# Where two batches' products wait between SBUF and DRAM, and which engine rounds weight blocks: one change to a three-stage kernel on one core

## The chip, the core and the metric

The kernel runs on one core of a Trainium2 chip. The metric is the device time of one execution in microseconds, the median of several. Five engines work side by side, each on its own list of instructions in order: PE (TensorE, the matrix products), ACT (ScalarE), DVE (VectorE), POOL (GpSimd) and SP (SyncE), which here issues every DMA.

## The reference

Three layers follow one another on 4 batches of 448 tokens.

- Attention with a sigmoid: `attn = sigmoid(q kT / 8 - log 448)` for 12 heads of 64, then `attn @ v`. The heads side by side give x, 1792 x 768.
- A gated product: `a = x @ w_a`, `b = x @ w_b` (both 768 x 1536), then `(a * b) @ w_out` (1536 x 768).
- Soft mixture of experts: `logits = x @ phi` (32 slots). A softmax over all tokens (`d`) mixes tokens into slots, 8 experts apply `relu(slot @ w1) @ w2`, and a softmax over the slots (`c`) gives the result, 1792 x 768.

The kernel never forms the second layer's output: it multiplies w_out with phi for the logits, and mixes the tokens of g = a * b into slots before w_out. So of g three things are needed per batch: g times (w_out phi), g with tokens on partitions, and the sum over tokens of `d` times g.

## The kernel before

**Stages.** Attention runs over 24 pairs of heads, six pairs a batch. While it runs, the weights are rebuilt from 64-bit words and written to DRAM as `ab32` and `out32`. Batch 0's product a * b (`ab(0)`) is woven into attention. Batches 1 and 2 are multiplied together by a scheme with 7 products in place of 8 (`unit(u)`, 12 units, line 682). Batch 3 follows in `ab(3)`, line 516. The tail reads out32 and the experts' weights w1 and w2 and ends with the output.

**Two roundings for each operand.** PE multiplies a number as a rounded high part and a remainder: an engine casts `t` to the high part, and another engine subtracts it from `t`. In the units `block` does this for the seven weight blocks (lines 571 and 572): even blocks are cast by DVE, odd ones by ACT, and POOL subtracts. `late_operands` (line 623) makes four operands at the start of the units; ACT casts and DVE subtracts (line 594). `last_x` does the same for batch 3's x, DVE casting, POOL subtracting (lines 633, 634).

**The last product, `ab(3)`.** It has 24 halves: 12 blocks of 128 columns, for w_a and then for w_b. A half is 18 matmuls on PE, in three steps of six. Its weight block comes from `ab32` (384 KB, `wr<-ab`) two halves ahead; DVE casts it (line 433), POOL subtracts (line 434), and the freed place lets SP issue the load of the block two halves later (line 425). At step 6, six steps into `ab(3)`, the pools of the units are closed and a pool `e1` of 17 load slots of 1 MB opens in their place; `pump` issues one load for the tail into the next open slot at every third step.

**g with tokens on partitions.** `group(b, gi)` (line 459) transposes a third of a batch's g into a tile. Batch 1 and 2 each own one half of `gk_01`; every third is written to DRAM (`gk32`, line 497) before the next third overwrites it. `reload_gk(b)` (line 500) reads the three thirds of one batch back into both halves of `gk_01` and into `gk_2`.

**The batch step `LG(b)`** (line 760) is a generator; PE's work is interrupted for one piece of it at a time, after a step of six matmuls. Its pieces are the logits (line 714), two token transposes (line 748) and `dg` (line 757), the sum over tokens. `LG(1)` and `LG(2)` run in `ab(3)`: the reload for batch 1 is asked for at step 12, that for batch 2 at the end of `LG(1)`, because both use the same tiles.

SP issues in program order. A DMA that waits for a tile to come free holds back all that stand behind it.

```
        for gi in range(3):
            t = (gk_01[:, gi] if gi < 2 else gk_2)[:T]
            sp.dma_start(out=t, in_=gk32[b - 1, gi])
```

Of the kernel before, what the change touches and what calls it, by code (L numbers as in the profile page):

```python
# [9 lines left out]
F32 = mybir.dt.float32  # L10
# [10 lines left out]
C = 4  # L21
T = S // C
# [4 lines left out]
NE1, NE2 = 17, 4  # L27
# [6 lines left out]
def body(ctx, tc, q, k, v, w_a, w_b, w_out, phi, w1, w2, out):  # L34
    nc = tc.nc
    pe, act, dve, pool, sp = nc.tensor, nc.scalar, nc.vector, nc.gpsimd, nc.sync
# [5 lines left out]
    gkp = ctx.enter_context(tc.tile_pool(name="gkp", bufs=1, side="left"))  # L42
# [5 lines left out]
    pools = {}  # L48
    drp = ctx.enter_context(tc.tile_pool(name="drp", bufs=1, space=bass.MemoryType.DRAM))
    psp = ps_ctx.enter_context(tc.tile_pool(name="psp", bufs=1, space=PSUM))  # L50

    run = {}
# [22 lines left out]
    gk_01 = lgp.tile([128, 2, 2048], F32, name="gk_01")  # L75
    gk_2 = gkp.tile([128, 2048], F32, tag="gkp0", name="gk_2")
# [10 lines left out]
    ab32 = drp.tile([KF, 2, 128, KD * 128], F32, name="ab32")  # L87
    out32 = drp.tile([128, KF, DM], F32, name="out32")
    clog32 = drp.tile([T, C, B, NS], F32, name="clog32")
    gk32 = drp.tile([2, 3, T, 2048], F32, name="gk32")  # L90

    idj = ident.rearrange("p (j s) -> p j s", j=4)
    small = gk_01.rearrange("p a n -> p (a n)")
# [104 lines left out]
    xt = {}  # L198
# [250 lines left out]
    gT, gtok, live = {}, {}, set()  # L449
# [9 lines left out]
    def group(b, gi, evac=(act.copy, dve.tensor_copy) * 2):  # L459

        if (b, gi) != (B - 1, 2):
            for _ in range(GDEL):
                yield
        lps = lp[b]
        t = ms()
        for j in range(4):
            fc = 4 * gi + j
            pe.matmul(t[32 * j:32 * j + 32], wphi[:, fc], gT[b, fc], start=True, stop=True)  # L468
        if gi == 0:
            act.copy(lps, t)  # L470
        else:
            dve.tensor_tensor(lps, lps, t, op=ALU.add)
        if (b, gi) == (B - 1, 2):
            gk = e2.tile([128, 2048], F32, tag="e20", name="gk_3")
        elif b in (1, 2):
            gk = gk_01[:, b - 1]
        else:
            gk = gk_01[:, gi] if gi < 2 else gk_2
        gkt = gk[:T]
        gk = gk[:T].rearrange("p (c n) -> p c n", c=C)  # L480
        if (b, gi) == (B - 1, 2):
            yield
        for c in range(C):
            tp = ms((T, 512))
            for i in range(4):
                pe.transpose(tp[:, i * 128:(i + 1) * 128],  # L486
                             gT[b, 4 * gi + i][:, c * T:(c + 1) * T], ident)
            evac[c](gk[:, c], tp)
            if c != 1 or (b, gi) == (B - 1, 2):
                yield  # L490
                if b < B - 1 and c < C - 1:
                    yield
        for i in range(4):
            gT.pop((b, 4 * gi + i))
            live.discard(b * KF + 4 * gi + i)
        if b in (1, 2):
            sp.dma_start(out=gk32[b - 1, gi], in_=gkt)
        gtok[b, gi] = gk

    def reload_gk(b):  # L500
        for gi in range(3):
            t = (gk_01[:, gi] if gi < 2 else gk_2)[:T]
            sp.dma_start(out=t, in_=gk32[b - 1, gi])
            gtok[b, gi] = t.rearrange("p (c n) -> p c n", c=C)

    def ab(b):
        for fc in range(KF):
# [58 lines left out]
    def block(u, m, t):  # L566
        q = (7 * u + m) % RING
        abt = {4: "wh0", 5: "wl0", 6: "wh1", 7: "wl1"}
        nm = abt.get(q, f"wx{q}")
        w = (abp if q in abt else pools["cp"]).tile([128, 2, BLK], F32R, tag=nm, name=nm)  # L570
        (act.copy if m % 2 else dve.tensor_copy)(w[:, 0], t)  # L571
        pool.tensor_tensor(w[:, 1], t, w[:, 0].bitcast(F32), op=ALU.subtract)  # L572
        wb_t[u, m] = w

# [16 lines left out]
    def split_x(nm, i, t, pl, names, rnd=None, sub=None):  # L591
        xh, xl = (pl.tile([128, S], F32R, tag=x, name=x) for x in names)
        (rnd or dve.tensor_copy)(xh, t)
        (sub or pool).tensor_tensor(xl, t, xh.bitcast(F32), op=ALU.subtract)
        xs[nm, i] = xh, xl
# [24 lines left out]
    def late_operands(nm):  # L620
        n = {"S3": NP, "S1": 2 * NP, "A22": 2 * NP + 3, "S4": NP + 3}[nm]
        for i in range(3):
            split_x(nm, i, xt[n + i], pools["xb"], (f"{nm}h{i}", f"{nm}l{i}"), act.copy, dve)

    def last_x():

        for kk in range(NP):
            g = 3 * NP + kk
            r = xt[g]
            xh = x1p.tile([128, S], F32R, tag=f"t{kk}", name=f"t{kk}")  # L630
            nm = f"t{kk + 5 if kk else 11}"
            xl = x1p.tile([128, S], F32R, tag=nm, name=nm)
            dve.tensor_copy(xh, r)
            pool.tensor_tensor(xl, r, xh.bitcast(F32), op=ALU.subtract)
            xt[g] = (xh, xl)
            yield
# [75 lines left out]
    def logits(b):  # L712
        lf, lps = ms(), lp[b]
        pe.matmul(lf, selF.rearrange("p j s -> p (j s)"), lps, start=True, stop=True)
        yield
        mx = col()
        dve.tensor_reduce(mx, lf, axis=AX.X, op=ALU.max)
        nm = col()
        if b:
            mn = col()  # L720
            dve.tensor_tensor(mn, run["m"], mx, op=ALU.max)
            mx, m0 = mn, run["m"]
        dve.tensor_scalar(nm, mx, -1.0, None, op0=ALU.mult)
        if b:
            dm = col()
            dve.tensor_tensor(dm, m0, mx, op=ALU.subtract)
        run["m"] = mx
        yield
        sm = col()
        ls, d = run["lsd"]  # L730
        act.activation(d, lf, AF.Exp, bias=nm, accum_out=sm)
        if b:
            al = col()
            act.activation(al, dm, AF.Exp)
            run["al"] = al
        act.copy(ls, lf)
        yield
        if b:
            sn = col()
            dve.scalar_tensor_tensor(sn, run["s"], al, sm, op0=ALU.mult, op1=ALU.add)  # L740
            sm = sn
        run["s"] = sm
# [7 lines left out]

    def dg(b, dtok, gp, groups):

        gk = gtok[b, 2][:, None] if groups == (2,) else gk_01[:T].rearrange("p g (c n) -> p g c n", c=C)
        o = gp.rearrange("p (g n) -> p g n", g=3)[:, groups[0]:groups[-1] + 1]
        for c in range(C):
            for j in range(4):
                pe.matmul(o[32 * j:32 * j + 32], dtok[:, c], gk[:, :, c, j * 128:(j + 1) * 128],  # L757
                          start=(c == 0), stop=(c == C - 1))

    def LG(b):  # L760
        t = run["lsd2"]
        run["lsd"] = t[:, :S], t[:, S:2 * S]
        dtok, ltok = (t[:T, i:i + C * NS].rearrange("p (c s) -> p c s", c=C) for i in (2 * S, 2 * S + C * NS))
        yield
        yield from logits(b)
        run["lg"] = b
        yield
        tokens(run["lsd"][0], ltok)
        sp.dma_start(out=clog32[:, :, b], in_=ltok)
        yield  # L770
        tokens(run["lsd"][1], dtok)
        yield
        gp = ms((128, FF // 4))
        for groups in ((0, 1), (2,)):
            dg(b, dtok, gp, groups)
        if b:
            dve.scalar_tensor_tensor(acc, acc, run["al"], gp, op0=ALU.mult, op1=ALU.add)
        else:
            dve.tensor_copy(acc, gp)
        yield  # L780
        if b == B - 3:
            reload_gk(b + 1)
        elif b == B - 2:
            run.pop("lsd2")
            open_slots(run["e1"], [1])
            open_slots(gkp, [0])

    def last_LG():

# [69 lines left out]
    def open_slots(pl, names):  # L859
        slots.extend((pl, f"{pl.name}{i}") for i in names)  # L860
# [104 lines left out]
    for i, frac in enumerate(ab(B - 1)):  # L965
        fc = i // 6
        if i < 6:
            fill_step()
        if i == 6:
            while fill:  # L970
                fill_step()
            cp_ctx.close()
            xb_ctx.close()
            e1 = run["e1"] = ctx.enter_context(tc.tile_pool(name="e1", bufs=1, side="right"))
            run["lsd2"] = e1.tile([128, 2048], F32, tag="e11", name="lsd2")
            run["wr"] = e1.tile([128, 2048], F32, tag="e10", name="wr")
            load_w(LAST + 6)
            load_w(LAST + 7)
            open_slots(e1, range(2, NE1))
            fill.append(LG(1))  # L980
            fill.append(LG(2))
        elif i == 12:
            reload_gk(1)
        if i > 6 and i % 3 == 1:
            pump()
    for kk in range(NP):
# [19 lines left out]
    for what in order0:  # L1006
        i = what[1]
        h, n, f0 = (0, 4, 4 * i) if i < 3 else (1, 6, 6 * (i - 3))
# [8 lines left out]
    for kk in range(0, KD, 2):  # L1017
        f = ms((128, 2, 256))
# [8 lines left out]
    for n in range(0, len(order1), 4):  # L1027
        _, g, x, _ = order1[n]
# [12 lines left out]
    for kk in range(0, KE, 2):  # L1041
        f = ms((128, 2, 256))
# [30 lines left out]
    for h in range(2):  # L1073
        for b in range(B):
            pl, nm = slots.pop(0)
# [4 lines left out]
    for h, (c0, w) in enumerate(COLS):  # L1080
# [4 lines left out]
        t = ms((128, w))  # L1085
        pe.matmul(t, selF.rearrange("p j s -> p (j s)"), s4[:, c0:c0 + w], start=True, stop=True)
        evac[h](s4r[:, c0:c0 + w], t)
        for c in range(C):
            op = []
            for b in range(B):  # L1090
                tag = tags[k % 6]
# [35 lines left out]
```

## Time and profile before

| | |
|---|---|
| median of 3 runs | 725.8 us (725.58 to 730.64) |
| the profiled execution's own time | 728.99 us |
| its span | 727.1 us |
| granted TensorE clock, mean | 0.975 |
| PE busy | 665.9 us (92%) |
| DVE, POOL, ACT busy | 392.3, 301.2, 285.2 us |
| the 16 DMA engines, mean share | 64.5% |

The profiled execution is 1.89 us longer than its span, and 3.2 us longer than the median. A busy PE is not a fast PE: its matmuls overlap, and the granted clock (1.0 stands for 2.4 GHz, 0.5 for 1.2 GHz) sets their pace. DMA shares are means over 16 engines and can read a few hundredths above 1.

### The profile page before, as it was taken

How to read it: one execution, taken by the hardware profiler on the slowest of the kernel's cores; microseconds unless marked ns; L12 is line 12 of the kernel's file. 1: busy time of each engine (PE TensorE's matmuls, PEld its weight loads, DVE VectorE, ACT ScalarE, POOL GpSimd, SP SyncE). 2: the span in 40 equal slices, each digit the busy share in tenths (PEclk: the TensorE clock that was granted, in tenths of full speed). 3: DMA queues.
4: the chain of work that ended last, by engine and by line, in shares of the span. 5: the costliest groups of instructions: out<-in, count | busy, mean ns of one | idle time of the engine just before them, and what ended most of it. 6: DMA issues, size and time to landing. Idle time of an engine off the chain costs nothing.

```text
span 727.1 us, 10908 instructions
## 1 busy us (share of the span) xinstructions
PE 665.9 (92%) x4123; PEld 473.6 (65%) x4123; DVE 392.3 (54%) x580; ACT 285.2 (39%) x503; POOL 301.2 (41%) x226
## 2 busy tenths in 40 slices
PE   6999998999999999999899999999299999998683
PEld 3547876776774545468788988988178987433131
DVE  4767897889725246249997887754022222300022
ACT  4987887877825666761113112103011011100021
POOL 0244677677634066016986676643124442100000
PEclk9999999999999899999999999999799999998898
DMA  9998998899624242101114313325998995999998
GB/s 205 254 285 210 290 322 295 248 305 279 218 66 147 55 102 64 57 0 45 45 44 137 95 49 106 121 81 157 286 276 316 356 345 202 365 415 416 410 356 258
DMA packets 105332, 150.58 MB, mean 207 GB/s; under 512 B 50944, under 2 KB 83968, under 8 KB 100864
## 3 DMA queue, kind: packets, MB, share of 16 engines
q1 hardware_dynamic: 105280, 149.89, 64.5%
q8 instruction: 33, 0.54, 0.3%
q14 instruction: 19, 0.16, 0.1%
HBM read 124.53 MB, written 25.34 MB: 206 GB/s over the span
## 4 chain that ended last, share of the span: by engine, by line
PE 71%; DMA 13%; DVE 9%; ACT 3%; issue 2%; SPq 0%; POOL 0%; ACTq 0%; DVEq 0%; POOLq 0%
PE ab L516 22%; PE sc L195 11%; PE sc L682 10%; DMA e<-in_moe_w 8%; PE sc L182 7%; PE ab L682 5%; PE ms L149 3%; PE ms L486 2%; DMA gk<-gk 2%; PE ms L757 2%; PE ab L182 1%; DMA ab<-w 1%; DMA gkp<-in_moe_w 1%; PE ms L468 1%; ACT a L185 1%
## 5 line engine op out<-in xcount | busy, mean ns | idle before, releaser
L339 POOL TENSOR_TENSOR w<-gk,cy 128x768 int32<-128x768 int32 x36 | 66.6, 1850 | 91.3 <-DVE gk L334 57.6
L185 ACT ACTIVATE a<-sc,sums 112x448 f32<-112x448 f32 x158 | 89.1, 645 | 14.0 <-PE sc L182 13.9
L195 PE MATMUL sc<-a,vn 112*64 112x448 f32 x384 | 77.8, 546 | 2.3 <-ACT a L185 2.3
L434 POOL TENSOR_TENSOR wl<-wr,wh 128x768 fp32r<-128x768 f32 x22 | 40.5, 1842 | 76.9 <-DVE wh L433 41.2
L516 PE MATMUL ab<-t,wh 128*128 128x448 f32 x288 | 64.9, 370 | 0.0
L516 PEld LDWEIGHTS ab<-t,wh 128*128 128x128 f32 x288 | 53.2, 188 | 4.6 <-issue 0.6
L195 PEld LDWEIGHTS sc<-a,vn 112*64 112x64 f32 x384 | 25.7, 136 | 40.5 <-issue 34.0
L434 POOL TENSOR_TENSOR wl<-w,wh 128x768 fp32r<-128x768 f32 x24 | 45.0, 1876 | 2.5 <-ACT wh L433 2.5
L1058 PE MATMUL ab<-e,gk 128*32 128x384 f32 x240 | 34.0, 558 | 9.8 <-DMA e<-in_moe_w 9.8
L332 DVE TENSOR_SCALAR mf<-gk 128x768 f32<-128x768 f32 x36 | 34.1, 946 | 16.4 <-ACT gk L321 16.4
L523 ACT COPY misc<-ab 128x448 f32<-128x448 f32 x24 | 12.9, 536 | 76.5 <-PE ab L516 76.5
L572 POOL TENSOR_TENSOR wx<-wr,wx 128x384 fp32r<-128x384 f32 x29 | 34.8, 1206 | 12.5 <-DVE wx L571 12.5
L571 ACT CAST wx<-T 128x384 fp32r<-128x384 f32 x23 | 11.5, 512 | 69.1 <-DVE T L587 42.1
L182 PE MATMUL sc<-qh,kh 64*112 64x448 f32 x158 | 36.5, 432 | 1.3 <-ACT qh L142 0.6
L526 DVE TENSOR_TENSOR misc<-misc,ab 128x448 f32<-128x448 f32 x24 | 14.8, 617 | 38.1 <-PE ab L516 38.1
L333 DVE TENSOR_SCALAR gk<-mf 128x768 uint32<-128x768 uint32 x36 | 34.3, 953 | 1.2
L516 PE MATMUL ab<-xh,wh 128*128 128x448 f32 x144 | 34.9, 378 | 0.0
L516 PE MATMUL ab<-xh,wl 128*128 128x448 f32 x144 | 34.5, 375 | 0.0
L516 PE MATMUL ab<-xl,wh 128*128 128x448 f32 x144 | 34.5, 375 | 0.0
L516 PE MATMUL ab<-t,wl 128*128 128x448 f32 x144 | 34.0, 371 | 0.0
L572 POOL TENSOR_TENSOR wx<-T,wx 128x384 fp32r<-128x384 f32 x23 | 25.3, 1102 | 16.0 <-ACT wx L571 16.0
L182 PE MATMUL sc<-qh,kl 64*112 64x448 f32 x158 | 31.8, 375 | 0.0
(421 smaller groups left out, 1455.9 us busy)
## 6 DMA issues: line engine op xcount, KB each, us to landing
e<-in_moe_w SPq DMA_DIRECT2D x23, 1024.0 KB, 7.5
e<-in_moe_w SPq DMA_DIRECT2D x23, 768.0 KB, 15.1
wr<-ab SPq DMA_DIRECT2D x14, 768.0 KB, 4.6
gk<-gk SPq DMA_DIRECT2D x12, 896.0 KB, 7.8
ab<-w SPq DMA_DIRECT2D x24, 384.0 KB, 7.2
wr<-ab SPq DMA_DIRECT2D x18, 384.0 KB, 5.4
kn<-in_k SPq DMA_DIRECT2D x48, 112.0 KB, 4.1
qn<-in_q SPq DMA_DIRECT2D x48, 112.0 KB, 4.1
```

Of the source, the lines that this page charges most:

```text
L149: pe.transpose(t[:, c * T:(c + 1) * T], a[:, c].rearrange("p h d -> p (h d)"), ident[:T, :T])
L182: pe.matmul(sc[h], kx[r, cs], qx[r], start=(i == 0), stop=(i == 2))
L185: act.activation(a, sc[h], AF.Sigmoid, bias=nlog[:T], scale=1.0 / math.sqrt(D))
L195: pe.matmul(pv_t[g][64 * h:64 * h + 64], qkv_t["v", g][:, h, c, :], a_t.pop((g, h, c)), start=(c == 0), stop=(c == C - 1))
L332: dve.tensor_scalar(mf, m, LOW, HIGH, op0=ALU.max, op1=ALU.min)
L333: dve.tensor_scalar(mi, mf.bitcast(U32), 3, 0x3FFFFFFF, op0=ALU.logical_shift_left, op1=ALU.bitwise_and)
L339: pool.tensor_tensor(thirds(w), m.bitcast(I32), thirds(cy_t.pop(x)), op=ALU.add)
L434: pool.tensor_tensor(wl, t, wh.bitcast(F32), op=ALU.subtract)
L516: pe.matmul(t, w[:, kk * 128:(kk + 1) * 128], xt[b * NP + kk][xi], start=(s == 0 and kk == 0), stop=(s == 2 and kk == KD - 1))
L572: pool.tensor_tensor(w[:, 1], t, w[:, 0].bitcast(F32), op=ALU.subtract)
L682: pe.matmul(t, w[:, wi, k * 128:(k + 1) * 128], xs[ORDER[m], k][xi], start=(s == 0 and k == 0), stop=(s == 2 and k == 2))
L1058: pe.matmul(sps[h][32 * j:32 * j + 32], hT[:, 2 * x + i, 2 * j + g], ring[order2[n + j]][0][:, i, c0:c0 + w], start=(g == 0 and x == 0 and ...
```

## The change

Of batches 1 and 2 the last third of g is no longer written to DRAM; it stays in that batch's half of `gk_01`, where `group` left it. The first two thirds of both batches are read back at step 6 of `ab(3)`, all four at once, into four load slots of `e1` (2 to 5). `dg` reads each third from where it lies, one third at a time for batches 1 and 2. `LG(1)` passes its turn three steps longer before its `dg`; `LG(0)` passes one turn more before its transposes. The four slots are opened for tail loads after `LG(1)` and `LG(2)`; the slot in `gkp` is opened early, at step 12. In the units ACT casts all seven blocks, in `last_x` too, and the remainders of A22 and S4 are subtracted by POOL.

```
-        if b in (1, 2):
+        if b in (1, 2) and gi < 2:
             sp.dma_start(out=gk32[b - 1, gi], in_=gkt)
...
-    def reload_gk(b):
-        for gi in range(3):
-            t = (gk_01[:, gi] if gi < 2 else gk_2)[:T]
-            sp.dma_start(out=t, in_=gk32[b - 1, gi])
-            gtok[b, gi] = t.rearrange("p (c n) -> p c n", c=C)
+    def reload_gk():
+        for b in (1, 2):
+            for gi in range(2):
+                nm = f"e1{2 * b + gi}"
+                t = run["e1"].tile([128, 2048], F32, tag=nm, name=nm)[:T]
+                sp.dma_start(out=t, in_=gk32[b - 1, gi])
+                gtok[b, gi] = t.rearrange("p (c n) -> p c n", c=C)
...
-        (act.copy if m % 2 else dve.tensor_copy)(w[:, 0], t)
+        act.copy(w[:, 0], t)
...
-            split_x(nm, i, xt[n + i], pools["xb"], (f"{nm}h{i}", f"{nm}l{i}"), act.copy, dve)
+            split_x(nm, i, xt[n + i], pools["xb"], (f"{nm}h{i}", f"{nm}l{i}"), act.copy, dve if nm in ("S3", "S1") else pool)
...
-            dve.tensor_copy(xh, r)
+            act.copy(xh, r)
...
         act.copy(ls, lf)
         yield
+        if not b:
+            yield
...
-        yield
+        for _ in range(4 if b == 1 else 1):
+            yield
         gp = ms((128, FF // 4))
-        for groups in ((0, 1), (2,)):
+        for groups in ((0,), (1,), (2,)) if b else ((0, 1), (2,)):
             dg(b, dtok, gp, groups)
...
         if b == B - 3:
-            reload_gk(b + 1)
+            open_slots(run["e1"], [2, 3])
         elif b == B - 2:
             run.pop("lsd2")
-            open_slots(run["e1"], [1])
-            open_slots(gkp, [0])
+            open_slots(run["e1"], [1, 4, 5])
...
             load_w(LAST + 7)
-            open_slots(e1, range(2, NE1))
+            reload_gk()
+            open_slots(e1, range(6, NE1))
             fill.append(LG(1))
             fill.append(LG(2))
         elif i == 12:
-            reload_gk(1)
+            open_slots(gkp, [0])
```

SP's list from the loads of step 6 on (`wr<-ab` is a weight block, `e<-out` a piece of out32 for the tail, `gk` and `e<-gk` the thirds of g, `clog` a small store). Before:

```order
L425 DMA wr<-ab_99 128x768 x2
L877 DMA e_5238<-out_100 128x4x512
L877 DMA e_5273<-out_100 128x4x512
L769 DMA clog_101<-lsd_5228 448x1x32
L503 DMA gk_93<-gk_102 112x2048 x2
L503 DMA gk_94<-gk_102 112x2048
L877 DMA e_5316<-out_100 128x4x512
L503 DMA gk_93<-gk_102 112x2048 x2
L503 DMA gk_94<-gk_102 112x2048
L425 DMA wr<-ab_99 128x768
```

The same place in the changed kernel:

```order
L425 DMA wr<-ab_99 128x768 x2
L505 DMA e_5230<-gk_102 112x2048
L505 DMA e_5232<-gk_102 112x2048
L505 DMA e_5234<-gk_102 112x2048
L505 DMA e_5236<-gk_102 112x2048
L881 DMA e_5244<-out_100 128x4x512
L881 DMA e_5279<-out_100 128x4x512
L773 DMA clog_101<-lsd_5226 448x1x32
L881 DMA e_5319<-out_100 128x4x512
L425 DMA wr<-ab_99 128x768
```

Four reloads stand where six stood, ahead of the out32 pieces and not behind them; the next weight block still has all of them in front of it.

PE's list around `dg` of `LG(1)` (line 757 before, 761 now). The rows of lines 516 and 518 are matmuls of `ab(3)`, named by the weight tile at their end. Before, in the middle of half 4:

```order
L516 MATMUL ab<-t_3831,wh_5253 128x448
L516 MATMUL ab<-t_3850,wh_5253 128x448
L757 MATMUL ms<-gk_93,lsd_5228 32x256 x16
L757 MATMUL ms<-gk_94,lsd_5228 32x128 x16
L516 MATMUL ab<-t_3747,wl_5254 128x448
```

Now, in the middle of half 5:

```order
L518 MATMUL ab<-t_3831,wh_5296 128x448
L518 MATMUL ab<-t_3850,wh_5296 128x448
L761 MATMUL ms<-e_5230,lsd_5226 32x128 x16
L761 MATMUL ms<-e_5232,lsd_5226 32x128 x16
L761 MATMUL ms<-gk_93,lsd_5226 32x128 x16
L518 MATMUL ab<-t_3747,wl_5297 128x448
```

Eighteen matmuls, one whole half, now stand between the old place and the new one. In the same way `dg` of `LG(2)` stands in half 8 and not in half 7.

POOL's list at the start of the units (a name that ends in l is a remainder). Before:

```order
L572 TENSOR_TENSOR wl_3618<-wr,wl_3618 128x384
L572 TENSOR_TENSOR wx_3647<-T_3615,wx_3647 128x384
L572 TENSOR_TENSOR wx_3673<-wr,wx_3673 128x384
L572 TENSOR_TENSOR wx_3687<-T_3616,wx_3687 128x384
```

Now:

```order
L574 TENSOR_TENSOR wl_3618<-wr,wl_3618 128x384
L596 TENSOR_TENSOR A22l_3636<-gk_93,A22h_3635 128x448
L596 TENSOR_TENSOR A22l_3640<-gk_93,A22h_3639 128x448
L596 TENSOR_TENSOR A22l_3644<-gk_93,A22h_3643 128x448
L574 TENSOR_TENSOR wx_3647<-T_3615,wx_3647 128x384
L596 TENSOR_TENSOR S4l_3662<-t_1803,S4h_3661 128x448
L596 TENSOR_TENSOR S4l_3666<-t_2096,S4h_3665 128x448
L596 TENSOR_TENSOR S4l_3670<-t_2425,S4h_3669 128x448
L574 TENSOR_TENSOR wx_3673<-wr,wx_3673 128x384
```

Six subtractions that were on DVE have come in among the weight blocks' own.

## Rows read from the trace of the kernel before

**Rows 1.** The page: busy time by engine; chain that ended last, by engine.

```profile
PE 665.9 (92%) x4123; PEld 473.6 (65%) x4123; DVE 392.3 (54%) x580; ACT 285.2 (39%) x503; POOL 301.2 (41%) x226
...
PE 71%; DMA 13%; DVE 9%; ACT 3%; issue 2%; SPq 0%; POOL 0%; ACTq 0%; DVEq 0%; POOLq 0%
```

**Rows 2.** Timeline of PE, 508 to 548: start, duration, line, operation, [idle before].

```profile
524.89 5.30 PE L757 MATMUL ms<-gk,lsd 112*32 112x256 f32 x64 [13.15 <-DMA gk<-gk]
...
541.86 2.88 PE L757 MATMUL ms<-gk,lsd 112*32 112x256 f32 x64
...
547.21 0.97 PE L516 MATMUL ab<-t,wh 128*128 128x448 f32 x4
```

**Rows 3.** Timeline of SP, 480 to 727: start, duration, DMA issued.

```profile
502.73 2.79 SPq L425 DMA_DIRECT2D wr<-ab  x2
...
509.84 2.14 SPq L503 DMA_DIRECT2D gk<-gk  x3
...
528.59 1.97 SPq L503 DMA_DIRECT2D gk<-gk  x3
...
533.55 0.34 SPq L425 DMA_DIRECT2D wr<-ab  x1
...
607.22 13.99 SPq L888 DMA_DIRECT2D e<-in_moe_w  x5
```

**Rows 4.** Windows: stretch, length, busy time of each engine, PEclk, DMA share, GB/s.

```profile
354.00:360.00 6.00, 3.52 (x16) 2.63 (x15) 5.93 (x7) 0.93 (x2) 4.91 (x5) 1.00 0.24 62
...
511.00:531.00 20.00, 6.85 (x72) 4.49 (x71) 0.74 (x2) 0.00 (x0) 0.65 (x1) 0.66 1.00 271
557.00:602.00 45.00, 45.00 (x234) 40.78 (x233) 12.34 (x21) 4.38 (x8) 20.29 (x11) 1.00 0.89 332
602.00:622.00 20.00, 17.57 (x144) 13.10 (x143) 5.60 (x15) 3.40 (x8) 6.49 (x15) 1.00 0.66 233
622.00:652.00 30.00, 29.07 (x261) 11.01 (x260) 4.82 (x9) 3.75 (x7) 0.00 (x0) 1.00 1.00 403
```

**Rows 5.** DMA issues in 528.5:530.4, in 533.5:533.6, in 547:547.2; last, us to landing.

```profile
gk<-gk SPq DMA_DIRECT2D x3, 896.0 KB, 10.6
...
wr<-ab SPq DMA_DIRECT2D x1, 384.0 KB, 10.8
...
wr<-ab SPq DMA_DIRECT2D x1, 384.0 KB, 4.5
```

**Rows 6.** Timeline of PE, 560 to 727: two neighbouring halves begin.

```profile
571.88 2.59 PE L516 MATMUL ab<-t,wh 128*128 128x448 f32 x12
...
575.53 2.60 PE L516 MATMUL ab<-t,wh 128*128 128x448 f32 x12
```

**Rows 7.** Timeline, 224 to 254: `LG(0)` in attention.

```profile
239.23 0.40 PE L748 MATMUL ms<-ident,ls_d 32*112 32x32 f32 x4 [1.72 <-ACT ls_d L736]
...
242.57 2.29 ACT L185 ACTIVATE a<-sc,sums 112x448 f32<-112x448 f32 x4
...
243.54 4.34 PE L757 MATMUL ms<-gk,ls_d 112*32 112x256 f32 x64
...
251.51 0.46 PE L182 MATMUL sc<-qh,kh 64*112 64x448 f32 x2
```

**Rows 8.** Groups of DVE and ACT, 312 to 490; of POOL, 200 to 490: busy, mean ns.

```profile
L571 DVE CAST wx<-wr 128x384 fp32r<-128x384 f32 x27 | 17.8, 664 | 0.0
L582 DVE TENSOR_TENSOR wr<-wr 128x384 f32<-128x384 f32 x11 | 13.8, 1256 | 0.4
...
L571 ACT CAST wx<-T 128x384 fp32r<-128x384 f32 x21 | 10.5, 513 | 66.1 <-DVE T L587 42.1 <-DVE T L583 24.0
...
L572 POOL TENSOR_TENSOR wx<-wr,wx 128x384 fp32r<-128x384 f32 x29 | 34.8, 1206 | 12.5 <-DVE wx L571 12.5
...
L594 POOL TENSOR_TENSOR A12l<-t,A12h 128x448 fp32r<-128x448 f32 x3 | 4.2, 1391 | 1.9 <-DVE A12h L593 1.9
...
L594 POOL TENSOR_TENSOR S2l<-s,S2h 128x448 fp32r<-128x448 f32 x3 | 3.4, 1142 | 1.5 <-DVE S2h L593 1.5
```

More of the change, by code (lines that the diff above doesn't have):

```diff
@@ L89, in body @@
     clog32 = drp.tile([T, C, B, NS], F32, name="clog32")
-    gk32 = drp.tile([2, 3, T, 2048], F32, name="gk32")
+    gk32 = drp.tile([2, 2, T, 2048], F32, name="gk32")
     idj = ident.rearrange("p (j s) -> p j s", j=4)
@@ L751, in dg @@
     def dg(b, dtok, gp, groups):
-        gk = gtok[b, 2][:, None] if groups == (2,) else gk_01[:T].rearrange("p g (c n) -> p g c n", c=C)
+        gk = gtok[b, groups[0]][:, None] if len(groups) == 1 else gk_01[:T].rearrange("p g (c n) -> p g c n", c=C)
         o = gp.rearrange("p (g n) -> p g n", g=3)[:, groups[0]:groups[-1] + 1]
```

## The prediction, as it was put on record

> **What bounds the kernel now.** The page comes first: PE is busy 92% of the span and carries 71% of the chain that ended last; DMAs carry 13% of it [rows 1]. So a change pays where PE stands still, or where the tail waits for its loads, and engine work beside a busy PE pays nothing. PE's timeline shows one large hole. In the last product, at `dg` of `LG(1)`, PE waits 13.15 us for a reloaded third of g and starts at 524.89 [rows 2]. The window around it shows a second cost: the granted clock is 0.66 on average there, so part of it at the lower level of 1.2 GHz, and 1.00 in the stretches behind it [rows 4]. The same 64 matmuls of `dg` take 5.30 us after the hole, and 2.88 us for `LG(2)` at 541.86 [rows 2]. What idled PE before the clock fell is that wait.
>
> SP's timeline shows why the wait is long: the three reloads are issued at 509.84, behind two weight blocks and two pieces of out32, some 2 us before PE needs them [rows 3]. DMA engines are full there (share 1.00, 271 GB/s) [rows 4]. The windows then show the rest: from 557 to 602 PE never stops and DMA has a tenth of its time free; from 602 to 622 a third of it; from 622 on it is full at 403 GB/s [rows 4]. The tail's next loads are issued at 607.22, when the last weight block gives its slot back [rows 3]. That is set by PE's progress, so what PE saves before 602 moves the whole tail.
>
> **The change, part by part.**
>
> *The wait for reloaded thirds goes.* The reloads leave as soon as the two weight blocks are out, which is at 505.5 (502.73 and 2.79) [rows 3]. Batch 1 needs two thirds, 1,792 KB. With the two blocks of 384 KB ahead that is 2.6 MB; at 271 GB/s 9.7 us, so they land at about 512.4 counted from 502.73, at 515.2 counted from 505.5. `dg` was asked for at 524.89 - 13.15 = 511.74 and is now asked for one half later; a half is 575.53 - 571.88 = 3.65 us [rows 6], so at 515.4. They are just in time: 13.15 us are saved, and with no hole before it `dg` runs at the full clock, 5.30 - 2.88 = 2.42 us more. Together 15.6. Batch 2's thirds follow and are needed a good 10 us later. `dg` in three narrow pieces has 96 matmuls in place of 64 over the same columns; I cost that at nothing, with 1.4 us for each of the two steps (half of 2.88 more) as the upper end.
>
> *What is late next: a weight block.* SP's list has the next weight block behind all four reloads and three pieces of out32. From 502.73 on the queue must move two blocks (768 KB), four thirds (3,584 KB), three pieces (128 x 4 x 512 floats, 1,024 KB each) and that block: 7,808 KB, 8.0 MB. At 271 GB/s, the rate of just such a mix, this takes 29.5 us: the block lands at 532.2. That a block waits its turn is seen now too: the one issued at 533.55 behind three reloads takes 10.8 us to land, one issued at 547 takes 4.5 [rows 5]. PE needs it for half 8. Half 8 starts at 547.21 now [rows 2]; take away 15.6 us, and 2.88 because `dg` of `LG(2)` moves behind its beginning, and it could start at 528.8. So a new wait of 3.4 us. The ends: at 332 GB/s, the rate of 557 to 602 [rows 4], the block is there at 526.8 and nothing is lost; if reloads run as the later three did (two of 896 KB in 10.6 us, 173 GB/s [rows 5]), it comes at 549 and 20 us are lost. I stay with 271, since 173 contains the start of an emptied queue. The remaining gain of the last product is 15.6 - 3.4 = 12.2. From half 10 on everything is as before, only earlier.
>
> *Does the tail keep it?* Between 511 and 622 the DMA engines are idle for 0.11 x 45 + 0.34 x 20 = 11.8 us [rows 4], and two reloads fall away, 1.8 MB or 6.8 us at 271 GB/s. That is 18.6 us of room, more than 12.2. The number of tail loads in `ab(3)` stays at 18; slots change names only. So the tail starts earlier by what PE saves. Two stores fewer are work beside a busy PE and count nothing.
>
> *Casts from DVE to ACT in the units.* 48 casts of the weight blocks leave DVE, where they take 664 ns on the mean, and cost ACT 513 ns each [rows 8], as do the six of `last_x`. ACT is busy 0.93 us in the six from 354 to 360, so it has the room [rows 4]. PE is what counts: it stands 6.00 - 3.52 = 2.48 us in that stretch, with DVE at 5.93 [rows 4]. I take 1.8 us of it as regained. Against it: six subtractions go to POOL, 1.14 us each when undisturbed (S2l), 1.39 beside DVE casts (A12l) [rows 8]. 6.9 us of work at the start of the units, ahead of the products that need them; the three of A22 fit in the time POOL would have waited, the three of S4 (3.4 us) do so in part. I take 1.0 us lost. Net gain 0.8; the ends are 2.5 gained, and 4.4 lost (all of 6.9 waited for, 2.5 regained).
>
> One rule of the Trainium skill speaks against this part. Its page "SBUF — State Buffer", section "Who interferes with whom", says that a DVE instruction with two inputs in SBUF and a GpSimd instruction that reads SBUF hold one port pair by turns, the second blocked until the first is done. The trace agrees: a DVE subtraction of two SBUF tiles (L582) takes 1.256 us on the mean where the cast of as many elements takes 0.664 [rows 8]. By the rule each of the six could wait for such an instruction too, 7.5 us more, and the sum below would be about 7 us. It is the third rival.
>
> *`LG(0)`.* PE waits 1.72 us for ACT's result, then `dg` takes 4.34 us [rows 7], more than the 2.88 at full clock. One more turn puts other matmuls ahead of the transposes, and the product that now ends at 251.51 ahead of `dg`. ACT still delivers at 239.2, and its four sigmoids end at 244.86 [rows 7], so not all of it goes. Between nothing and 1.72 + 1.46 = 3.2 us I take 1.2.
>
> **The sum** is 12.2 + 0.8 + 1.2 = 14.2 us. The profiled execution, 728.99 us with 1.89 us outside the span, would take 714.8. It lies 3.2 us above the median of 725.8; on the median's scale the forecast is **711.6**.
>
> **Rivals.**
>
> 1. *The weight blocks are later than I think.* The reload's own rate is below 271, so that half 8 waits 8 to 12 us. For it: 173 GB/s for the later three. Against it: 271 GB/s with a full queue contains the first three. The gain is 15.6 - 10 + 2.0 = 7.6, the time 718.2 (716 to 720). Chance 0.14.
> 2. *No new wait.* The queue has no store of a third in it any more at 502, and reloads ahead of everything run faster: at 332 GB/s the 3.4 us go, and PE may regain all of 2.48 and 3.2. Time 725.8 - 15.6 - 2.5 - 3.2 = 704.5 at the best; around 707. Chance 0.13.
> 3. *POOL and DVE block each other at the start of the units.* The six subtractions take 7.5 us more between them, PE waits for S4, and the sum falls to about 7: 719. For it: 1.39 and 1.256 us [rows 8]. Against it: DVE loses its casts there. Chance 0.06.
> 4. *The change doesn't do what it says:* the thirds are not back when `dg` asks, since their slots lie where the units' last readers work, and SP stands before them. The wait stays whole; only it then also covers the weight block. Time 725. Chance 0.04.
> 5. *Slower: POOL sets the pace of the units.* All low parts now hang on POOL behind ACT's queue, and two units hold 14 subtractions of blocks and 2 products on POOL. A unit is 63 matmuls, at the 3.65 us for 18 of [rows 6] 12.8 us. If POOL's instruction took over 25.6 / 16 = 1.6 us on the mean, PE would wait in every unit; at 2.48 us a unit, the hole of 354 to 360 repeated in 11 units, 27.3 us are lost: 725.8 - 12.2 - 1.2 + 27.3 = 739.7. It decides against the change from 13.4 / 11 = 1.2 us a unit on. Against it: POOL's rows stand at 1.14 to 1.39 us, and it is busy 4.91 of 6 us in the worst stretch. Chance 0.05.
>
> **Numbers.** The forecast case has what is left, 0.58: 708 to 716 about 711.6. About 1%, 7.3 us, is what a measurement of this kernel can tell from no change: the line lies at 718.5. Below it are the forecast, the second rival, and half each of the first and third: 0.58 + 0.13 + 0.07 + 0.03 = 0.81. Within 1%: the rest of those two and the fourth, 0.07 + 0.03 + 0.04 = 0.14. Slower: 0.05. The range takes in the second rival's middle and the first rival's whole, 706 to 720; the fourth, the fifth and the tails of the second and third stay outside.
>
> **What would show it.** *Right:* no wait of PE at `dg` in half 5 over 1 us, `dg` near 2.9 us, granted clock 1.00 from 511 to 531; a wait of a few us before half 8, with the landing of the first weight block behind the reloads as its end; `ab(3)` from its first matmul to its last some 12 us shorter; the load that is issued at 607.22 now issued near 593. *Wrong:* a wait at half 8 over 8 us, or the clock falling there, gives the first rival; waits of PE for POOL in units past the third give the fifth; a tail in which PE no longer waits for loads, or starts them no earlier, breaks the step that hands the gain on to the end. I would be wrong as a whole if reloads still landed after 520.

## The result, and the profile after

The changed kernel takes **717.16 us** (median of 4 runs, 715.64 to 718.24) beside 727.68 for the kernel before, measured with it: ratio 0.9851, 95% interval [0.9804, 0.9898]. Measured a second time it took 718.03 beside 726.29: 0.9896 [0.9859, 0.9933]. It is faster, by 10.5 and 8.3 us, 1.0 to 1.5%. The forecast was 711.6 in a range of 706 to 720: the sign and the range hold, the likeliest number is about 6 us too good. On the forecast's own scale, a kernel before of 725.8 us, the two ratios give 715.0 and 718.3; the forecast case was to lie between 708 and 716, the first rival between 716 and 720. The profiled execution after is 717.61 us with a span of 715.6 (before 728.99 and 727.1).

The page after, busy time by engine and the chain that ended last by engine, answers to [rows 1]:

```profile
PE 663.9 (93%) x4187; PEld 476.7 (67%) x4187; DVE 358.9 (50%) x520; ACT 307.9 (43%) x557; POOL 303.2 (42%) x232
...
PE 77%; DMA 11%; DVE 4%; ACT 3%; POOL 2%; issue 1%; SPq 1%; ACTq 0%; DVEq 0%; POOLq 0%
```

DVE gives 33 us of busy time away, ACT takes 23, and POOL, absent from the chain before, now holds 2% of it. PE's timeline in the last product answers to [rows 2] (start, duration, line, operation, idle before):

```profile
513.51 1.96 PE L761 MATMUL ms<-e,lsd 112*32 112x128 f32 x64
515.28 1.06 PE L761 MATMUL ms<-gk,lsd 112*32 112x128 f32 x32
...
530.97 2.61 PE L518 MATMUL ab<-t,wh 128*128 128x448 f32 x6 [4.31 <-DVE wh L433]
533.51 2.84 PE L761 MATMUL ms<-e,lsd 112*32 112x128 f32 x64
536.17 1.05 PE L761 MATMUL ms<-gk,lsd 112*32 112x128 f32 x32
```

The hole of 13.15 us is gone: `dg` of `LG(1)` starts at 513.51 without a wait and takes 1.96 + 1.06 us. In its place stands a wait of 4.31 us before half 8, for the rounding of a weight block. Behind it the same `dg` of `LG(2)` takes 2.84 us for the 64 matmuls that took 1.96 before it. The windows show why (stretch, length, busy times, granted clock, DMA share, GB/s):

```profile
353.00:359.00 6.00, 6.00 (x31) 5.53 (x30) 3.74 (x7) 1.58 (x5) 6.00 (x7) 1.00 0.46 132
511.00:528.00 17.00, 15.65 (x161) 13.30 (x159) 3.07 (x7) 2.20 (x6) 3.68 (x2) 1.00 1.03 317
528.00:534.00 6.00, 3.03 (x18) 2.28 (x22) 2.08 (x6) 0.00 (x0) 1.83 (x1) 0.55 1.02 336
534.00:540.00 6.00, 6.00 (x106) 5.51 (x99) 1.27 (x3) 0.12 (x1) 1.89 (x2) 0.89 0.99 364
```

The granted clock is 1.00 through the place of the old hole and 0.55 behind the new wait, so most of that stretch is at 1.2 GHz. The first line is the stretch of units that had 2.48 us of idle PE [rows 4]: it is full now. SP's timeline, and below it one issue of the weight block with its time to landing, answer to [rows 3, 5]:

```profile
500.89 0.80 SPq L425 DMA_DIRECT2D wr<-ab  x2
501.73 1.85 SPq L505 DMA_DIRECT2D e<-gk  x4
...
507.33 7.53 SPq L773 DMA_DIRECT2D clog<-lsd  x1
...
517.99 1.45 SPq L425 DMA_DIRECT2D wr<-ab  x1
...
596.03 0.33 SPq L892 DMA_DIRECT2D e<-in_moe_w  x1
```

```profile
wr<-ab SPq DMA_DIRECT2D x1, 384.0 KB, 12.2
```

The block that half 8 needs lands at 517.99 + 12.2 = 530.2. The tail's loads begin at 596.03 in place of 607.22, 11.2 us earlier: the tail keeps what PE saves.

**Where the time went**, by stretches of PE's timeline, between starts of the same matmuls (us). `LG(0)` is the stretch of attention that holds it, matmuls 192 to 256 of the value products; "half 0-11" runs from the start of half 0 of the last product to the start of half 11, "tail" from there to the end. The kernels of the next section stand beside the two.

```
                     LG(0)  units 0-2  units 3-5  units 6-11  half 0-11  tail
before               38.85    47.23      44.96      82.62       73.83   166.17
changed              38.15    47.56      44.03      82.62       64.46   165.80
changed, again       39.76    46.13      43.93      82.61       66.47   166.15
reload only          38.85    47.25      44.99      82.62       63.91   165.86
engines only         38.85    47.66      43.92      82.62       73.95   165.50
A22, S4 on DVE       39.63    47.29      44.03      82.62       66.11   165.78
pieces later         39.75    47.55      44.03      82.62       59.00   165.56
... and old start    38.25    44.99      44.03      82.62       59.23   165.29
... and old LG(0)    38.80    45.04      44.03      82.62       58.14   166.42
pieces, LG(1) early  39.10    47.60      44.03      82.61       63.55   165.58
second batch later   39.78    47.60      44.04      82.61       67.22   165.85
old start, a turn    39.52    44.99      43.92      82.62       58.14   167.39
```

What lies ahead of these stretches has no edit, and differs by up to 2.6 us between profiles; so single spans are not compared to the microsecond, stretches are.

### The profile page after: what moved, and what is told of

The parts are those of the page before. It is cut to its first block, busy times and chain, and to the rows that moved or that the text cites. A ratio compares the mean times of both kernels' runs of the same rounds, so it can differ in the third digit from the quotient of the medians.

```text
span 715.6 us, 11048 instructions
## 1 busy us (share of the span) xinstructions
PE 663.9 (93%) x4187; PEld 476.7 (67%) x4187; DVE 358.9 (50%) x520; ACT 307.9 (43%) x557; POOL 303.2 (42%) x232
## 4 chain that ended last, share of the span: by engine, by line
PE 77%; DMA 11%; DVE 4%; ACT 3%; POOL 2%; issue 1%; SPq 1%; ACTq 0%; DVEq 0%; POOLq 0%
PE ab L518 23%; PE sc L684 13%; PE sc L195 10%; DMA e<-in_moe_w 9%; PE sc L182 7%; PE ab L684 7%; PE ms L149 3%; PE ms L486 2%; DMA wr<-ab 2%; PE ab L182 1%; PE ms L468 1%; PE ms L761 1%; PE ms L377 1%; PE ms L364 1%; DVE gk L334 1%
## 5 line engine op out<-in xcount | busy, mean ns | idle before, releaser
L1063 PE MATMUL ab<-e,gk 128*32 128x384 f32 x240 | 32.9, 521 | 12.4 <-DMA e<-in_moe_w 12.4
L1063 PEld LDWEIGHTS ab<-e,gk 128*32 128x32 f32 x240 | 9.6, 114 | 34.7 <-DMA e<-in_moe_w 23.9
L528 DVE TENSOR_TENSOR misc<-misc,ab 128x448 f32<-128x448 f32 x24 | 14.8, 616 | 35.0 <-PE ab L518 35.0
```

Of the source, the lines that this page charges most:

```text
L1063: pe.matmul(sps[h][32 * j:32 * j + 32], hT[:, 2 * x + i, 2 * j + g], ring[order2[n + j]][0][:, i, c0:c0 + w], start=(g == 0 and x == 0 and ...
```

## Experiments

A ratio is always to the kernel before as it ran on the same chip: 724.9 us beside the first four kernels below, 726.29 beside the next three, 726.92 beside the two after them, and 726.29 again beside the changed kernel.

**The parts alone.** Two kernels, each with half of the change:

```diff
 # reload only: the changed kernel with
-        act.copy(w[:, 0], t)
+        (act.copy if m % 2 else dve.tensor_copy)(w[:, 0], t)
 # late_operands and last_x as before, no added turn in LG(0)

 # engines only: the kernel before with
-        (act.copy if m % 2 else dve.tensor_copy)(w[:, 0], t)
+        act.copy(w[:, 0], t)
 # late_operands and last_x as changed
```

> 

> The reload part alone: thirds that stay, four load slots, later dg of LG(1); the roundings, the subtractions of A22 and S4 and LG(0) are as in the kernel before. Theory: nearly all of the gain is in the last product, so 9.4 us less than before (the last product's own share in the two profiles), a ratio of 0.987, and the wait before half 8 stays near 4.3 us. Rival: the engines' part carries some of it, because fewer DVE instructions in the units let the last product start earlier; then this kernel gains 7 us or less and the next one 3 or more.

> 

> The engines' part alone: block and last x roundings on ScalarE, subtractions of A22 and S4 on POOL; reloads and LG(0) as before. Theory: what is lost at the start of the units (3.5 us in the profiles) and what is regained at the hole of 354 to 360 and later (3.9 us) cancel: 0.4 us less than before, within 1 us either way, a ratio of 0.998 to 1.001. Rival: the loss at the start is chance of that one profiled run and not of the change; then 3 us less than before.

Reload only: 718.3 us, 0.9904 [0.9873, 0.9936]; the last product's halves take 9.9 us less, with a wait of 3.4 us before half 8. So the expected 9.4 us are in that stretch, while the times show about 7 us and the expected 0.987 lies at the edge of the interval. Engines only: 726.21 us, 0.9999 [0.9972, 1.0025]; 0.4 us lost in units 0 to 2, 1.0 us regained in units 3 to 5. The second theory holds, and the rival, which wanted 3 us or more from the engines, falls. The gain is the reload's; the engines' part is worth nothing that a time can show. Whether the third that stays or the early issue of the others brings more was not tried apart.

**What is lost at the start of the units.** In the changed kernel PE's waits in the first three units, by what ended them (total, times, longest, us), are:

```profile
PE ab L684 <- POOL S4l L596: 2.0, 3, 0.9
PE sc L684 <- POOL A22l L596: 0.9, 1, 0.9
```

The second was there in the kernel before too, 0.9 us for A22l, then made by VectorE; the first is new. They look like POOL's price, so the six subtractions went back to VectorE.

```diff
-            split_x(..., act.copy, dve if nm in ("S3", "S1") else pool)
+            split_x(..., act.copy, dve)
```

> 

> The changed kernel with the six subtractions of A22 and S4 back on VectorE; all else as changed. Theory: the start of the units loses 3.5 us because PE waits for three subtractions of 1.22 us (S4) and three of 1.44 us (A22) on POOL, and the clock falls behind these waits; with them on VectorE 2 to 3.5 us come back: 714 to 715 us against 717.2, ratio to before near 0.982. Rival: VectorE is as late with them, since its casts gone are outweighed by these six, or the waits move to the product behind; then within 1 us of the changed kernel.

719.18 us, 0.9914 [0.9886, 0.9942]: no gain, and units 0 to 2 take 47.29 us, within 0.3 of the 47.56 of the changed kernel. The theory fell, the rival holds. VectorE's own three subtractions of S4 show why; first in this kernel, then in the kernel before (DVE's timeline):

```profile
327.31 3.58 DVE L596 TENSOR_TENSOR S4l<-t,S4h 128x448 fp32r<-128x448 f32 x3
```

```profile
327.97 1.68 DVE L594 TENSOR_TENSOR S4l<-t,S4h 128x448 fp32r<-128x448 f32 x3
```

The same three take more than twice as long. POOL's timeline of the first of these kernels shows what ran beside them:

```profile
326.34 1.38 POOL L574 TENSOR_TENSOR wx<-wr,wx 128x384 fp32r<-128x384 f32 x1 [0.51 <-ACT wx L573]
327.68 1.40 POOL L574 TENSOR_TENSOR wx<-T,wx 128x384 fp32r<-128x384 f32 x1
329.03 1.38 POOL L574 TENSOR_TENSOR wx<-wr,wx 128x384 fp32r<-128x384 f32 x1
```

In the kernel before POOL ran nothing from 326.5 to 330.0, because it waited for roundings that VectorE had yet to do (POOL's timeline of the kernel before):

```profile
325.20 1.30 POOL L572 TENSOR_TENSOR wx<-T,wx 128x384 fp32r<-128x384 f32 x1 [1.63 <-ACT wx L571]
330.00 1.02 POOL L572 TENSOR_TENSOR wx<-wr,wx 128x384 fp32r<-128x384 f32 x1 [3.50 <-DVE wx L571]
```

ScalarE rounds at once, so POOL subtracts at once, beside VectorE, and both are slow: 1.38 us for POOL's, which took 1.02 in the changed kernel at 325.87, beside VectorE instructions that read a product's result, and 0.99 at 330.46 beside an idle VectorE. This agrees with the Trainium skill, "SBUF — State Buffer", section "Who interferes with whom": a VectorE instruction with two inputs in SBUF and a GpSimd instruction that reads SBUF keep each other waiting. The test of this is the old start.

**The weight block's place in the queue.** The pieces of out32 that stand ahead of the third weight block are loaded from turn 16 on, and the block goes out directly behind the reloads.

```diff
-        if i > 6 and i % 3 == 1:
+        if i > 15 and i % 3 == 1:
             pump()
```

> 

> The changed kernel with the loads for the tail starting at turn 16 of the last product in place of turn 7, so that the third weight block stands directly behind the four reloads and not behind three pieces of out32 as well. Theory: the block lands some 10 us earlier, near 520, the 4.3 us wait before half 8 goes and with it the fall of the clock (2.2 us); the tail keeps it: 6.5 us less than the changed kernel, 710.7 us, ratio to before 0.976. Rival 1: the block's landing is set by the queue that SP itself is stuck behind, whatever follows the reloads; the wait stays over 3 us and the time within 1 us of the changed kernel. Rival 2: the wait goes, but the pieces moved back (3 MB) take the DMA time that the tail's loads had, and the tail gives back what is gained: within 2 us of the changed kernel, with longer waits for loads behind 600.

711.06 us, 0.9819 [0.9792, 0.9845]. All that PE waits for in the last product up to 560 is one line:

```profile
PE ms L761 <- DMA e<-gk: 0.7, 1, 0.7
```

The wait before half 8 is gone and the clock stays at 1.00 from 502 to 602; the halves take 59.00 us, 5.5 and 7.5 less than in the two profiles of the changed kernel, and the tail keeps it. The block landed 10.6 us after its issue at 515.10, at 525.7 rather than near 520, and still before it was needed: 22.8 us after the first block's issue at 502.88, where the 4,792 KB up to it make 18.1 us at 271 GB/s. The time is the expected one; the expected ratio, 0.976, is not, since the kernel before is 2.8 us faster on this chip than beside the first run of the changed kernel. By the stretches the theory holds, and both rivals fall.

**The old start of the units, and the old `LG(0)`.** Both on top of the later pieces:

```diff
 # old start
-        act.copy(w[:, 0], t)
+        (act.copy if m % 2 or u > 2 else dve.tensor_copy)(w[:, 0], t)
 # and subtractions of A22 and S4 on VectorE
 # old LG(0), on top
-        if not b:
-            yield
```

> 

> The changed kernel with the pieces loaded later (as in the run before this one that did so), and the start of the units as in the kernel before: blocks of units 0 to 2 are rounded by ScalarE and VectorE in turn, the subtractions of A22 and S4 are on VectorE; from unit 3 on all roundings are ScalarE's. Theory: the 3.5 us lost at the start come from POOL: when ScalarE rounds at once, POOL subtracts at once, and then three subtractions of S4 take 3.6 us on either engine, where VectorE took 1.68 us with POOL idle. With the old start the stretch from the first product of unit 0 to that of unit 3 takes 44 us (47.2 before, 47.6 changed), so 3.4 us less than the run with later pieces alone: ratio to before 0.977. Rival: the gain of unit 2 hangs on the early blocks, so the hole at 354 to 360 comes back when the start is as before: 47.2 us again, no gain.

> 

> As the run with the old start of the units and later pieces, but LG(0) too as in the kernel before, without the added turn. Theory: the added turn is worth nothing on the mean: the 32 groups of attention from number 192 to 256 of the value products took 38.85 us in three profiles without it, and 38.15, 39.75 and 39.63 with it, as the clock fell for a shorter or a longer stretch behind the same waits. So 38.85 here, and 0 to 1 us less than the run beside it. Rival: the added turn gains the 1.2 us of the prediction and the two longer profiles are chance: 1.2 us slower than the run beside it.

With the old start: **708.65 us** (707.28 to 710.26), 0.9762 [0.9735, 0.9788], with the next one the fastest; units 0 to 2 take 44.99 us, 2.6 less, where 3.4 were expected. DVE's timeline, and POOL's beside it:

```profile
326.63 1.68 DVE L596 TENSOR_TENSOR S4l<-t,S4h 128x448 fp32r<-128x448 f32 x3
```

```profile
328.66 1.01 POOL L574 TENSOR_TENSOR wx<-wr,wx 128x384 fp32r<-128x384 f32 x1 [3.50 <-DVE wx L573]
```

With the blocks' roundings in VectorE's queue again, POOL waits for them, and VectorE's subtractions are back at 0.56 us each, and the wait for S4 is no longer among PE's waits. Units 3 to 5 keep the gain of the change. With the old `LG(0)` as well: 708.7 us, 0.9766 [0.9721, 0.9810], and 38.80 us in its stretch. Without the turn four profiles give 38.80 to 38.85, with it eight give 38.15 to 39.78, 39.24 on the mean. The added turn gains nothing.

**The three turns of `LG(1)`.**

```diff
-        for _ in range(4 if b == 1 else 1):
+        for _ in range(1):
```

> 

> The changed kernel with the pieces loaded later, and without the three added turns in LG(1), so that dg is asked for half a block earlier, near 511.5, when the second third has not landed (517.2 there). Theory: the turns are part of what removes the hole: without them PE waits 3 to 6 us at dg and the clock falls behind it; 4 to 8 us slower than the run with later pieces, ratio to before 0.987 to 0.993. Rival: the early issue alone removes the hole, dg in three pieces runs as its thirds land, with under 1.5 us of waits; same time as the run with later pieces, ratio 0.982.

716.33 us, 0.9859 [0.9830, 0.9889]; halves 0 to 11 take some 4.5 us more than with the later pieces alone. PE's waits up to 560, and the window at `dg`:

```profile
PE ms L761 <- DMA e<-gk: 3.5, 2, 2.6
```

```profile
513.00:522.00 9.00, 6.41 (x77) 5.58 (x78) 1.08 (x2) 0.53 (x1) 1.36 (x1) 0.81 0.77 189
```

The ratio is just under the expected 0.987 to 0.993, the wait is the expected one. A part of the old hole is back, and the granted clock of that stretch is 0.81 on the mean. The early issue needed the later request too, as the theory had it.

**Only the order of the queue.** The changed kernel, with batch 2's thirds behind the weight block:

```diff
 # reload_gk takes the batch
-            reload_gk()
+            reload_gk(1)
...
+        elif i == 18:
+            reload_gk(2)
```

> 

> The changed kernel (pieces from turn 7 on) with batch 2's two thirds reloaded at turn 18 of the last product, behind the third weight block, in place of turn 6. Theory: what stands ahead of a transfer in the queue sets its landing. 1,792 KB fewer stand ahead of the block, 6.8 us at 271 GB/s, so it lands at about 524.4 and not 531.2, and the wait of 4.3 to 5.4 us before half 8 goes. But batch 2's thirds now have block, pieces and the next block ahead of them and land near 535, where dg of LG(2) asks at 529: a new wait of 4 to 7 us there, with the clock falling behind it; time within 3 us of the changed kernel, ratio to before 0.983 to 0.991. Rival: the three pieces of out32 are what is slow, whatever else stands there: the wait before half 8 stays over 3 us.

720.82 us, 0.9918 [0.9888, 0.9949], just outside the expected ratio. The block was issued at 514.07; its landing, and PE's two waits in the last product:

```profile
wr<-ab SPq DMA_DIRECT2D x1, 384.0 KB, 10.4
```

```profile
533.63 1.93 PE L760 MATMUL ms<-e,lsd 112*32 112x128 f32 x32 [4.36 <-DMA e<-gk]
...
537.21 1.94 PE L760 MATMUL ms<-e,lsd 112*32 112x128 f32 x32 [1.64 <-DMA e<-gk]
```

It lands at 524.5 (expected 524.4) and half 8 doesn't wait; `dg` of `LG(2)` waits 6.0 us instead (expected 4 to 7). What stands ahead in the queue sets who waits, as the theory says. Of the two orders tried, the one that moves the pieces back takes the wait away, since nobody asks for them soon; the one that moves the thirds back hands it on.

**One turn more**, on top of the old start, for the second third that lands 1.0 us late there:

```diff
-        for _ in range(4 if b == 1 else 1):
+        for _ in range(5 if b == 1 else 1):
```

> 

> The run with later pieces and the old start of the units, with four added turns in LG(1) in place of three. Theory: the second third lands 1 us after dg asks for it there, so one turn more (some 1.2 us of other matmuls) takes that wait away and no other comes: 0 to 1 us less, ratio to before 0.975, no wait of PE over 0.5 us in the last product. Rival: the later end of LG(1) delays LG(2) and the slots that it frees for the tail's loads: 1 to 3 us slower.

711.03 us, 0.9779 [0.9750, 0.9807], not told apart from 0.9762. PE's wait goes and the halves take 58.14 us, 1.1 less, but the tail takes 167.39, 2.1 more: no gain, and nearer the rival than the theory. The same is seen with the old `LG(0)`: 58.14 and 166.42. From half 0 to the end the four kernels with later pieces and `LG(1)` in time take 224.56, 224.52, 224.56 and 225.53 us. What PE saves past that is given back in the tail, where PE's waits for the experts' weights are 12.6 us in these two and 11.1 with the old start alone; by which transfer is not shown.

**The changed kernel again**, for one chip:

> 

> The changed kernel itself, beside the variants of this call, so that they are compared on one chip: ratio to before 0.985, a wait of 3 to 6 us before half 8 of the last product.

0.9896 was measured, so the gain is a third smaller than expected, and the wait was 5.4 us.

## Why the prediction was right, and where its number was off

- **The hole at `dg`:** right. Predicted 15.6 us from the wait and the clock; halves 0 to 11 take 15.7 us less in the two kernels in which PE waits for nothing there (73.83 to 58.14), and 14.8 with later pieces alone, where 0.7 us of wait are left. It was just in time: the second third landed at 513.25 (issued at 502.20, 11.05 us), and `dg`, which reads the first third first, began at 513.51. From the first block's issue at 500.89 that is 12.4 us where 9.7 were worked out, so blocks and reloads came at 212 GB/s and not at 271. The three narrow pieces cost nothing, as assumed: 513.51 to 516.34 is 2.83 us, beside 2.88. Without the later request there is a wait, as the kernel with `LG(1)` early shows.
- **The new wait before half 8:** the mechanism was right and its term too small. The block was to land 29.5 us after the first issue; it took 530.2 - 500.9 = 29.3, and 28.4 to 31.5 in the four profiles with three pieces and four thirds ahead of it, so the close hit is in part luck. The rate of 271 GB/s is a mean of two: in the nine profiles in which the four thirds are asked for at once, the two blocks and the thirds (4,352 KB) take 19.1 to 22.4 us, 199 to 233 GB/s; the pieces, the store and the block behind them (3,512 KB, in four profiles) take 9.1 to 10.2 us, 354 to 396 GB/s. The wait was put at 3.4 us; the four profiles show 4.3, 5.4, 3.4 and 6.2, longer the later the block lands. Of each, 0.7 us is the block's rounding between its landing (530.23) and the first matmul (530.97), which the prediction left out. **The step that failed is the sum behind it: the wait was counted bare, with no clock behind it.** Beside the 58.14 us without a wait, the two profiles of the changed kernel lose 6.3 and 8.3 us there, of which 4.3 and 5.4 are the wait itself and 2.0 and 2.9 the lower clock behind it. The hole's clock was counted as a gain, 2.42 us, and the same fall behind the new hole was not counted as a loss. "The clock falling there" was named in the prediction as the mark of its first rival, and the measured times lie by that rival's, 718.2; its own wait of 8 to 12 us did not come. That the total stayed in the range is then no proof of the sum.
- **Casts and units:** 0.8 us predicted, 0.6 found in the profile of the engines' part alone (0.4 lost, 1.0 regained) and in one of the changed kernel, 2.1 in the other. The places were right, both sizes were not: units 0 and 1 take 3.5 us more than before (34.7 beside 31.2), where 1.0 was predicted, and unit 2 takes 3.2 and units 3 to 5 take 0.9 less, where 1.8 was. In the second profile units 0 and 1 lose only 2.0: PE's waits there are the same, but the clock stayed up behind them (last section). The third rival's mechanism is real, at a third of the price it was given: beside POOL a VectorE subtraction takes 1.2 us rather than 0.56. In the changed kernel it is a part only. Of POOL's three subtractions for S4 two take 1.16 and 1.13 us beside VectorE instructions that read a product's result, the third 1.45 beside one with both inputs in SBUF. The prediction's row for this, 1.256 beside 0.664, sets a subtraction against a cast; the cleaner pair in the same trace is two subtractions of VectorE, 1.25 us at 322.72 beside POOL and 0.56 at 324.01 with POOL idle.
- **`LG(0)`:** 1.2 us predicted, 0.7 gained in one profile, 0.9 lost in the next, -0.4 on the mean of eight. PE's timeline after, in that stretch:

```profile
238.34 0.40 PE L752 MATMUL ms<-ident,ls_d 32*112 32x32 f32 x4 [1.11 <-ACT ls_d L738]
...
240.28 0.98 PE L182 MATMUL sc<-qh,kh 64*112 64x448 f32 x2 [1.01 <-ACT a L185]
...
242.90 4.37 PE L195 MATMUL sc<-a,vn 112*64 112x448 f32 x16
247.20 2.81 PE L761 MATMUL ms<-gk,ls_d 112*32 112x256 f32 x64
```

The wait of 1.72 us became 1.11 and 1.01, and the slow clock moved from `dg` (4.34 to 2.81 us) to the value products ahead of it (4.37 us here, 3.23 for the next 16; granted clock 0.72 from 243 to 247, 1.00 from 247 to 250). The prediction took the 1.46 us of slow `dg` as within reach without asking what would run in its place.
- **The tail keeps it:** right, with a tail of 165.80 us beside 166.17. Of the 11.2 us by which its loads come earlier 9.4 are the last product's; in this profile the last product also began 1.8 us earlier. It stops being true near 224.5 us from half 0 to the end.
- **The sum:** 14.2 us were predicted. The three terms measured are 9.4 + 0.6 + 0.7 = 10.7 us in one profile of the changed kernel and 7.4 + 2.1 - 0.9 = 8.6 in the other; most of what is missing is the last product's.
- **POOL as the pace of the units:** did not come; units 6 to 11 take 82.62 us in every kernel.

## What to carry to other kernels

Where a stall is taken away, price the next one with the clock that falls behind it, as you priced the first. Add up the bytes that stand ahead of each small load that PE waits for, and take the rate from the same kind of transfers: at 271 GB/s the sum came within 2 us of the landing while the pieces stood in the queue, and was 4.7 us short (18.1 beside 22.8) once they were gone and the slower thirds were left. Then move back what nobody needs soon: with the pieces moved the time was 0.9819 of that before, with thirds that were soon needed 0.9918, beside 0.9851 and 0.9896 with neither. When work is moved off a slow engine, ask who now runs at the same time: VectorE was fast here because POOL was still waiting for it.

## What was not expected of the hardware

- **An issue can itself be stuck.** SP took 7.53 us to issue a 56 KB store at 507.33, behind four thirds and two pieces, and 2.98 us for the piece after it; in the three other profiles with this queue the store took 8.02 to 9.76 us. With the pieces loaded later the same store took this (SP's timeline):

```profile
509.33 0.60 SPq L773 DMA_DIRECT2D clog<-lsd  x1
```

Two megabytes fewer were under way there. Whether it is bytes, packets or transfers that fill up was not tried.
- **Behind a row of short waits the clock may fall or not.** At the start of the units of the changed kernel the waits in a row are 0.94, 0.40, 0.62 and 0.94 us, and the granted clock of the six microseconds around the last of them reads 0.72, so part of them ran at 1.2 GHz:

```profile
329.00:335.00 6.00, 4.92 (x15) 4.22 (x16) 3.02 (x4) 0.92 (x2) 6.00 (x7) 0.72 0.00 1
```

In the same kernel's second profile the same four waits are 0.94, 0.38, 0.62 and 0.93 us, and the clock did not fall:

```profile
330.00:336.00 6.00, 4.55 (x21) 3.97 (x22) 3.62 (x4) 2.05 (x5) 6.00 (x6) 1.00 0.00 1
```

What decides between the two is not shown. It makes 1.4 us of difference in units 0 to 2 (47.56 and 46.13), so one profile is not enough to price such a row of waits.
